# Last two weight pairs of a gated layer applied group by group, four weight conversions moved to earlier pairs

## The chip, the cores and the metric

The kernel runs on one core of one Trainium2 chip. The metric is the device time of one execution in microseconds (us). The kernel before takes 609.58 us, the median of three runs (609.0 to 614.15).

The engines are called by what they do: TensorE (PE in the rows; PEld is its loading of weights) multiplies matrices, VectorE (DVE), ScalarE (ACT) and GpSimd (POOL) work on elements, and SyncE (SP) starts transfers.

## The reference

Attention, a layer of eight experts and a gated layer follow one another. The change is in the last:

```python
def _moe2_ref(x, w_a, w_b, w_out) -> np.ndarray:
    a = x @ w_a
    b = x @ w_b
    return (a * b @ w_out).astype(np.float32)
```

`x` has 1536 tokens of 512, `w_a` and `w_b` are 512 x 1536, `w_out` is 1536 x 512. The weights come as float64 numbers.

## The kernel before

The attention and the experts fill the first 275 us or so of the span, and the change does not touch them. What follows is the gated layer.

**Numbers in two parts.** Each operand of a product is held as a high and a low part (`abh` and `abl` for the weights of a pair, `gh` and `gl` for the gated values, the even and odd `yw` tiles for tokens and for the last matrix). A product takes three matmuls for one: high by high, high by low, low by high.

**Pairs.** The inner width of 1536 is cut into 12 pieces of 128, `fc` from 0 to 11. A pair is the piece of `w_a` and the piece of `w_b`. `product(fc, g)` applies a pair to a third of the tokens (group `g`, 512 tokens): 24 matmuls of 128 x 512, first the `w_a` half, then the `w_b` half. Its lines are L1116 and L1117 (both with `abh`) and L1118 (with `abl`). ScalarE copies the first half out (`asb`, L1121), VectorE multiplies the second half by it (`gt`, L1122).

**Conversions.** `load_w` turns 128 x 512 weights from float64 into the two parts. It is a generator that is advanced a step at a time by `some(steps, n)` or to its end by `run(steps)`. Its steps are: issue the next transfer on SP's queue (L1006); `c_rest` on ScalarE (L1016) and `c_top` on VectorE (L1018, L1020); `c_ex` and `c_top` on VectorE (L1024, L1026); the high part on ScalarE (L1029), `c_ex` on VectorE (L1030), `c_rest` times `c_ex` on POOL (L1031); a subtraction on VectorE (L1033) and the low part on POOL (L1034). The step that ends a conversion and the first of the next one are made in one advance, so a conversion in a chain takes four. Two conversions make a pair (`load_ab`, both side by side); twelve make the last matrix (`load_c`, three chunks of four).

**Places.** The chunks of the last matrix go to the `yw` tiles: chunk 0 to tiles 6 and 7, which are free, chunk 1 to tiles 0 and 1, chunk 2 to 2 and 3. Tiles 0 and 1 hold the tokens of group 0, tiles 2 and 3 those of group 1, until the last product of that group is done.

**Order.** Everything here stands under a manual schedule: each engine executes in the order of the code. The loop over `fc` from 1 to 11 (L1158) makes three products, and behind each advances four steps of what pair `fc + 1` needs; from `fc + 1 = 8` on a conversion of chunk 0 is chained behind these. In the loop of `fc = 11` the eight conversions of chunks 1 and 2 begin behind the product of group 1.

**Last product.** It has 36 positions (`order`): for each a group and an `fc`. `split_g` makes `gh` on ScalarE (L1155) and `gl` on VectorE (L1156), two positions ahead; there are three buffers of each. Behind the split two steps of the remaining conversions are advanced, and then twelve matmuls stand on TensorE: L1185 and L1186 with `gh`, L1187 with `gl`, four times. Positions 0 to 15 are the groups 0 and 1 with chunks 0 and 1 of the last matrix (position 8 is the first that reads chunk 1), positions 16 to 23 the same groups with chunk 2, the last twelve are group 2.

Of the kernel before, what the change touches and what calls it, by code (L numbers as in the profile page):

```python
# [23 lines left out]
P = 128  # L24
# [37 lines left out]
def _consts():  # L62
    """Shape-only constants, one [128, n] float32 array; name -> (offset, width)."""
    p = np.arange(P)
# [37 lines left out]
def fused_kernel(  # L102
# [64 lines left out]

    # ---------------------------------------------------------------- expert blocks
    slots = [(0, i, wa_p) for i in range(NSA)]
    tick = [0]  # L170

    def take(dt, prefer=None):
        """A tile in the place that has been free for longest, of the pool that is preferred if it has any."""
        slots.sort(key=lambda t: t[:2])
        n = next((n for n, t in enumerate(slots) if t[2] is prefer), 0)
        _, i, pool = slots.pop(n)
        return (i, pool), pool.tile([P, CH], dt, name=f"w{i}")
# [6 lines left out]
    def gather_chunk(wi, c, prefer=None):  # L184
        """A chunk of an expert's weights, as it is."""
        place, r = take(F32, prefer)
        nc.gpsimd.indirect_dma_start(
            out=r, out_offset=None, in_=wt, in_offset=bass.IndirectOffsetOnAxis(ap=wi(c), axis=0))
        return place, r

    def parts(chunk, held, prefer=None):
        """Tiles for the two parts of a chunk, and what makes a piece of them."""
        place, r = chunk
# [32 lines left out]
    def gather(wi, ti, n, prefer=(None, None)):  # L226
        """What a block of n times 128 tokens needs."""
        ws = [gather_chunk(wi, c, prefer[0]) for c in range(2)]
        xgs = gather_x(xs, ti, n)
        return ws + [gather_chunk(wi, c, prefer[1]) for c in range(2, NCH)], xgs  # L230
# [53 lines left out]
    def block(ws, xgs, dst, **where):  # L284
        """A block by itself."""
        x = split_x(xgs, **where)
# [9 lines left out]
    def block_then(ready, dst, after, beside, prefer, after_prefer):  # L296
        """A block whose tokens and first chunks are ready, with what makes those of the block after it ready."""
        ws, w, x, held = ready
# [27 lines left out]
    def half_block(ready):  # L326
        """128 tokens: the tokens are stationary in the first product, and its result is turned."""
        ws, w, (xh, xl), held = ready
# [21 lines left out]

    # ---------------------------------------------------------------- attention and routing
    def rpool(stack, name, bufs):
# [160 lines left out]
    def first_max(L, n, O, key):  # L513
        """One-hot over E of the first largest of L ([P, n, E]); key: 8 less its place."""
        mx = r_p.tile([P, n], F32, name=f"mx{n}")
# [16 lines left out]
    def turned(b, t2):  # L532
        """The tokens of two tiles to DRAM, and turned."""
        x = xt2[b, t2]
# [10 lines left out]
    def partial_logits(b, t2):  # L545
        """Each part of the sum in 32 rows of its own."""
        pa = ps_b.tile([P, KD, P], F32, name="pl4", tag="b").rearrange("p c i -> p (c i)")[:, :2 * P]
# [16 lines left out]
    def prefix(b):  # L564
        """How many tokens of each expert come before each token."""
        O = oh[:, b * RB:(b + 1) * RB, :]
# [7 lines left out]
    def places(b):  # L574
        """Each token's place among those of its expert: unit of 128, and a row of ohl; in steps."""
        t0 = b * RB
# [19 lines left out]
    def count(t):  # L596
        """How many of the first t tiles' tokens each expert has."""
        pn = bank(E)
# [10 lines left out]
    def rows_of(key, out):  # L609
        """Rows of the weights of expert 8 - key."""  # L610
        w0 = r_p.tile([P, 1], F32, name="w0")
# [3 lines left out]
    def of_expert(name, vec, t0, n):  # L615
        """The entry of vec ([P, E]) of each token's expert."""
        t3 = r1.tile([P, n, E], F32, name=name + "3")
# [5 lines left out]
    def rows_y(tf, n, a, b):  # L623
        """Rows of the tokens tf (from 1; 0 for none) in ya and yb; those not there have row p, kept for that."""
        d = r1.tile([P, n], F32, name=f"d{n}")
# [17 lines left out]
    def early_expert():  # L643
        """A block of tokens of the first TE tiles, of the expert that has most of them."""
        ce = ear["ce"] = counted(ear["pc"], "ce")
# [45 lines left out]
    def tables(pc, pn, other):  # L691
        """The experts of the blocks, and which unit of which block each token has; other runs between."""
        full = ear["full"]
# [162 lines left out]
    def step(n):  # L856
# [3 lines left out]
        def due(ahead):  # L860
            """The pair that begins in so many steps (the first one's turn comes a step late)."""
            m = n + ahead
            return begin.get(0 if m == 1 else m) if m else None
# [80 lines left out]

    # ---------------------------------------------------------------- the other blocks
    nrun = nc.values_load(nmax[0:1, 0:1], min_val=0, max_val=NJ,
# [16 lines left out]

    # ---------------------------------------------------------------- second layer
    NG = 3
# [18 lines left out]
    def turn_y(g, ys):  # L984
        yh, yl = yt[g] = yw_tile(2 * g, [P, KD, GT]), yw_tile(2 * g + 1, [P, KD, GT])
        for c in range(KD):
# [5 lines left out]
            nc.vector.tensor_tensor(out=yl[:, c, :], in0=px, in1=f(yh[:, c, :]), op=ALU.subtract)  # L992

    loads = []
    for fc in range(KF2):
        loads += [(wab, 2 * fc + ab) for ab in range(2)]
        if fc >= KF2 - CH // RW:
            loads.append((wc, fc - KF2 + CH // RW))
    loads += [(wc, n) for n in range(CH // RW, KF2 * DM // RW)]
# [9 lines left out]
    def load_w(src, n, hi, lo):  # L1009
        """RW float64 weights, as the bits they come in, to the two parts of their float32 values; in steps."""  # L1010
        fetch()
# [34 lines left out]
    def run(steps):  # L1046
        for _ in steps:
            pass
# [21 lines left out]
    with tc.manual_schedule():  # L1070
# [86 lines left out]

        for fc in range(1, KF2):  # L1158
            steps = iter(())
            if fc + 1 < KF2:  # L1160
                steps = load_ab(fc + 1)
                if fc + 1 >= KF2 - CH // RW:
                    steps = chain(steps, load_c(0, fc + 1 - KF2 + CH // RW))
            for g in range(NG):
                product(fc, g, acc)
                if fc == KF2 - 1 and g > 0:
                    split_g(g - 1)
                some(steps, 4 if fc + 1 < KF2 else 3)
                if fc == KF2 - 1 and g == 0:
                    steps = chain(*(load_c(1, n) for n in range(CH // RW)), *(load_c(2, n) for n in range(CH // RW)))  # L1170
            if fc + 1 < KF2:
                run(steps)

# [21 lines left out]
def layout(q, k, v, moe_w_gate, moe_w1, moe_w2, moe2_w_a, moe2_w_b, moe2_w_out):  # L1195
    """The inputs as the kernel reads them: reordered, repeated and padded, nothing else."""
    f = np.float32
# [42 lines left out]
```

## Time and profile before

| what | us |
|---|---|
| median of three runs (lowest, highest) | 609.58 (609.0, 614.15) |
| span of the profiled execution, first to last instruction | 592.6 |
| whole time of the profiled execution | not on the page |
| TensorE busy in the span | 564.9 (95%) |
| VectorE busy | 391.0 (66%) |
| ScalarE busy | 236.5 (40%) |
| POOL busy | 226.8 (38%) |
| share of TensorE in the chain that ended last | 60% |
| share of VectorE in that chain | 8% |

The span is what the trace covers; the rest of the time lies around it. The busy shares are means over stages with different limits. A row of a timeline gives the start, the duration, the engine, the line and operation, and in brackets how long the engine had been idle before it and what it had waited for. Matmuls are pipelined: each is shown with some 0.39 us, but the next one starts 0.23 us later, so starts are compared.

### The profile page before, as it was taken

The page shows a single profiled execution, that of the slowest core. Times are in us where ns is not written, and L with a number is a line of the kernel's source. Part 1 is how long each engine was busy: PE and PEld are TensorE (multiplying, and loading weights), DVE is VectorE, ACT ScalarE, POOL GpSimd, SP SyncE. Part 2 cuts the span into 40 slices and gives each one's busy share as a digit, 9 for nine tenths or more (in the row PEclk, how much of TensorE's full clock was granted, in tenths as well). Part 3 has the DMA queues.
Part 4 walks back from the last instruction along what each step waited for, and adds up shares of the span by engine and source line. Part 5 has one row for each costly group of instructions (what it writes and reads, how often), then busy time and mean ns, then how long its engine had stood idle before and what let it go on. Part 6 is the DMA issues. An engine that isn't in the chain of part 4 may idle for free.

```text
span 592.6 us, 8797 instructions
## 1 busy us (share of the span) xinstructions
PE 564.9 (95%) x3166; PEld 475.0 (80%) x3166; DVE 391.0 (66%) x924; ACT 236.5 (40%) x500; POOL 226.8 (38%) x196
## 2 busy tenths in 40 slices
PE   5999998879999999999999999999999998999997
PEld 4999897768998998987888888888888876668885
DVE  4655578785878869766555555567898578883321
ACT  3566654314755756563422122212233233332221
POOL 4332236734455756730013344444544533430000
PEclk9999999879999999999999999999999999999999
DMA  9997947124977858654311122222332212201101
GB/s 232 246 230 191 241 139 280 72 105 136 384 270 312 304 207 310 234 203 162 112 64 35 44 72 71 72 71 72 107 107 76 67 56 87 72 0 72 71 1 71
DMA packets 24414, 83.85 MB, mean 141 GB/s; under 512 B 2992, under 2 KB 5552, under 8 KB 20784
## 3 DMA queue, kind: packets, MB, share of 16 engines
q1 hardware_dynamic: 14112, 38.16, 22.8%
q0 software_dynamic: 6944, 38.80, 17.3%
q10 hardware_dynamic: 3312, 6.29, 3.1%
q8 instruction: 26, 0.43, 0.3%
q14 instruction: 20, 0.16, 0.1%
HBM read 69.72 MB, written 12.32 MB: 138 GB/s over the span
## 4 chain that ended last, share of the span: by engine, by line
PE 60%; DVE 8%; issue 4%; ACT 1%; DMA 1%; SPq 0%; ACTq 0%; DVEq 0%
PE pa L1118 11%; PE pa L1116 11%; PE pa L1117 11%; PE po L1187 3%; PE po L1186 3%; PE po L1185 3%; PE py L253 3%; PE py L254 3%; PE py L252 3%; PE ph L277 2%; PE ph L278 2%; PE ph L279 2%; DVE w L205 2%; DVE gl L1156 1%; DVE c_top L1026 1%
## 5 line engine op out<-in xcount | busy, mean ns | idle before, releaser
L1116 PE MATMUL pa<-yw,abh 128*128 128x512 f32 x288 | 113.7, 395 | 0.0
L1118 PE MATMUL pa<-yw,abl 128*128 128x512 f32 x288 | 112.8, 392 | 0.0
L1117 PE MATMUL pa<-yw,abh 128*128 128x512 f32 x288 | 112.1, 389 | 0.0
L1031 POOL TENSOR_TENSOR c_rest<-c_rest,c_ex 128x512 f32<-128x512 f32 x36 | 54.7, 1531 | 147.0 <-DVE c_ex L1030 146.9
L205 DVE TENSOR_TENSOR w<-w,w 128x512 fp32r<-128x512 f32 x96 | 68.1, 752 | 5.4 <-ACT w L204 4.5
L1122 DVE TENSOR_TENSOR gt<-pa,asb 128x512 f32<-128x512 f32 x36 | 24.8, 690 | 63.0 <-PE pa L1118 55.9
L1118 PEld LDWEIGHTS pa<-yw,abl 128*128 128x128 f32 x288 | 54.0, 188 | 13.0 <-POOL abl L1034 0.9
L457 PE MATMUL s<-kt,qd 128*128 128x120 f32 x192 | 57.0, 445 | 7.2 <-DMA qd<-in_q 7.2
L1117 PEld LDWEIGHTS pa<-yw,abh 128*128 128x128 f32 x288 | 54.1, 188 | 11.4
L1187 PE MATMUL po<-yw,gl 128*128 128x512 f32 x144 | 58.1, 404 | 4.8 <-DVE gl L1156 4.8
L1116 PEld LDWEIGHTS pa<-yw,abh 128*128 128x128 f32 x288 | 54.1, 188 | 10.8
L457 PEld LDWEIGHTS s<-kt,qd 128*128 128x128 f32 x192 | 53.2, 367 | 10.1 <-POOL kt L449 7.8
L204 ACT CAST w<-w 128x512 fp32r<-128x512 f32 x96 | 54.4, 616 | 5.9 <-DVE w L205 3.0
L1185 PE MATMUL po<-yw,gh 128*128 128x512 f32 x144 | 56.7, 394 | 0.0
L1186 PE MATMUL po<-yw,gh 128*128 128x512 f32 x144 | 56.6, 393 | 0.0
L277 PE MATMUL ph<-xh,w 128*128 128x256 f32 x192 | 55.8, 291 | 0.3 <-PEq L948 0.3
L278 PE MATMUL ph<-xl,w 128*128 128x256 f32 x192 | 55.2, 287 | 0.0
L279 PE MATMUL ph<-xh,w 128*128 128x256 f32 x192 | 54.9, 286 | 0.0
L1156 DVE TENSOR_TENSOR gl<-gt,gh 128x512 fp32r<-128x512 f32 x36 | 29.6, 826 | 36.2 <-ACT gh L1155 36.2
L1121 ACT COPY asb<-pa 128x512 f32<-128x512 f32 x36 | 21.0, 583 | 56.8 <-PE pa L1118 56.8
L252 PE MATMUL py<-w,hh 128*128 128x512 f32 x104 | 41.8, 402 | 0.0
L253 PE MATMUL py<-w,hh 128*128 128x512 f32 x104 | 41.2, 396 | 0.6 <-DVE w L205 0.6
(200 smaller groups left out, 1088.2 us busy)
## 6 DMA issues: line engine op xcount, KB each, us to landing
raw<-in_wab SPq DMA_DIRECT2D x22, 512.0 KB, 4.4
raw<-in_wc SPq DMA_DIRECT2D x12, 512.0 KB, 3.5
vt<-in_v SPq DMA_DIRECT2D x8, 585.0 KB, 7.2
kr<-in_k SPq DMA_DIRECT2D x8, 400.0 KB, 7.2
vbt<-in_vb SPq DMA_DIRECT2D x8, 390.0 KB, 5.9
qd<-in_q SPq DMA_DIRECT2D x16, 192.0 KB, 6.1
xs<-x ACTq DMA_DIRECT2D x12, 256.0 KB, 4.5
yg<-ya SPq DMA_DIRECT2D x8, 256.0 KB, 3.3
```

What stands on the lines that cost most here:

```text
L205: nc.vector.tensor_tensor(out=l[:, c], in0=r[:, c], in1=f(a[:, c]), op=ALU.subtract)
L252: nc.tensor.matmul(py, a, b_, start=(fc == 0), stop=False)
L277: nc.tensor.matmul(ph, a, xh[:, c, :], start=(c == 0), stop=False)
L278: nc.tensor.matmul(ph, a, xl[:, c, :], start=False, stop=False)
L279: nc.tensor.matmul(ph, l, xh[:, c, :], start=False, stop=(c == KD - 1))
L457: nc.tensor.matmul(s[:, w, :], qs[b, c][:, :, 4 * t2 + w], kts[i][:, w, :], start=True, stop=True)
L1116: nc.tensor.matmul(pa, a, yh[:, c, :], start=(c == 0), stop=False)
L1117: nc.tensor.matmul(pa, a, yl[:, c, :], start=False, stop=False)
L1118: nc.tensor.matmul(pa, l, yh[:, c, :], start=False, stop=(c == KD - 1))
L1185: nc.tensor.matmul(po[g][i], a, bh, start=(fc == 0), stop=False)
L1186: nc.tensor.matmul(po[g][i], a, bl, start=False, stop=False)
L1187: nc.tensor.matmul(po[g][i], l, bh, start=False, stop=(fc == KF2 - 1))
```

## The change

Lines of the new kernel are one higher than the old ones from L994 on to L1157, and ten higher behind the changed loop: the subtraction L1033 is L1034 there, POOL's addition L1034 is L1035, `gt` is L1123, `gl` L1157.

The loop over `fc` ends at 9. The last two pairs, `f0 = 10` and `f1 = 11`, are applied in the order (10,0), (10,1), (11,0), (11,1), (10,2), (11,2) instead of pair by pair. The weights of pair 11 are converted from ahead of (10,0) to behind (10,1). The conversions of chunks 1 and 2 begin behind (11,0). The four conversions of chunk 0 move from pairs 8 to 11 to pairs 3, 5, 7 and 9. The number of instructions on each engine stays the same in this layer.

```diff
+    early_c = list(range(3, KF2 - 2, 2))
     loads = []
     for fc in range(KF2):
         loads += [(wab, 2 * fc + ab) for ab in range(2)]
-        if fc >= KF2 - CH // RW:
-            loads.append((wc, fc - KF2 + CH // RW))
+        if fc in early_c:
+            loads.append((wc, early_c.index(fc)))
...
-        for fc in range(1, KF2):
-            steps = iter(())
-            if fc + 1 < KF2:
-                steps = load_ab(fc + 1)
-                if fc + 1 >= KF2 - CH // RW:
-                    steps = chain(steps, load_c(0, fc + 1 - KF2 + CH // RW))
+        f0, f1 = KF2 - 2, KF2 - 1
+        for fc in range(1, f0):
+            steps = load_ab(fc + 1)
+            if fc + 1 in early_c:
+                steps = chain(steps, load_c(0, early_c.index(fc + 1)))
             for g in range(NG):
                 product(fc, g, acc)
-                if fc == KF2 - 1 and g > 0:
-                    split_g(g - 1)
-                some(steps, 4 if fc + 1 < KF2 else 3)
-                if fc == KF2 - 1 and g == 0:
-                    steps = chain(*(load_c(1, n) for n in range(CH // RW)), *(load_c(2, n) for n in range(CH // RW)))
-            if fc + 1 < KF2:
-                run(steps)
+                some(steps, 4)
+            run(steps)
+        steps = load_ab(f1)
+        some(steps, 2)
+        for g in range(2):
+            product(f0, g, acc)
+            some(steps, 2)
+        run(steps)
+        product(f1, 0, acc)
+        steps = chain(*(load_c(c, n) for c in (1, 2) for n in range(CH // RW)))
+        some(steps, 2)
+        product(f1, 1, acc)
+        some(steps, 4)
+        for n, fc in enumerate((f0, f1)):
+            product(fc, 2, acc)
+            split_g(n)
+            some(steps, 5)
```

How this moves instructions is seen at three places.

TensorE, kernel before, where the second product of pair 10 ends and the third begins (`abh_4852` and `abl_4853` are the parts of pair 10; `yw2` to `yw5` are the tokens of groups 1 and 2):

```order
L1116 MATMUL pa_5027<-yw2_3683,abh_4852 128x512
L1117 MATMUL pa_5027<-yw3_3684,abh_4852 128x512
L1118 MATMUL pa_5027<-yw2_3683,abl_4853 128x512
L1116 MATMUL pa_5057<-yw4_3758,abh_4852 128x512
L1117 MATMUL pa_5057<-yw5_3759,abh_4852 128x512
L1118 MATMUL pa_5057<-yw4_3758,abl_4853 128x512
```

TensorE, changed kernel, behind the same second product (`abh_4882` and `abl_4883` are the parts of pair 10, `abh_4972` and `abl_4973` those of pair 11; `yw0` and `yw1` are the tokens of group 0):

```order
L1117 MATMUL pa_5042<-yw2_3683,abh_4882 128x512
L1118 MATMUL pa_5042<-yw3_3684,abh_4882 128x512
L1119 MATMUL pa_5042<-yw2_3683,abl_4883 128x512
L1117 MATMUL pa_5062<-yw0_3602,abh_4972 128x512
L1118 MATMUL pa_5062<-yw1_3603,abh_4972 128x512
L1119 MATMUL pa_5062<-yw0_3602,abl_4973 128x512
```

The product that follows (10,1) now reads pair 11, where it read pair 10.

VectorE, kernel before, from the middle of the conversions of pair 11 to the end of pair 10 (`gt_3671` is pair 10; the last conversion of chunk 0 stands behind the two subtractions):

```order
L1030 TENSOR_SCALAR c_ex<-c_top 128x512 x2
L1122 TENSOR_TENSOR gt_3671<-pa,asb 128x512
L1033 TENSOR_TENSOR c_top<-c_top,abh 128x512 x2
L1018 TENSOR_SCALAR c_top<-raw 128x512
L1020 SCALAR_TENSOR_TENSOR c_top<-raw,c_top 128x512
L1024 TENSOR_SCALAR c_ex<-raw 128x512
L1026 SCALAR_TENSOR_TENSOR c_top<-c_ex,c_top 128x512
L1122 TENSOR_TENSOR gt_3671<-pa,asb 128x512
```

VectorE, changed kernel, the same conversions (`gt_3671` is pair 10, groups 0 and 1; `gt_3672` is pair 11):

```order
L1123 TENSOR_TENSOR gt_3671<-pa,asb 128x512
L1025 TENSOR_SCALAR c_ex<-raw 128x512
L1027 SCALAR_TENSOR_TENSOR c_top<-c_ex,c_top 128x512
L1025 TENSOR_SCALAR c_ex<-raw 128x512
L1027 SCALAR_TENSOR_TENSOR c_top<-c_ex,c_top 128x512
L1031 TENSOR_SCALAR c_ex<-c_top 128x512 x2
L1123 TENSOR_TENSOR gt_3671<-pa,asb 128x512
L1034 TENSOR_TENSOR c_top<-c_top,abh 128x512 x2
L1123 TENSOR_TENSOR gt_3672<-pa,asb 128x512
L1019 TENSOR_SCALAR c_top<-raw 128x512
L1021 SCALAR_TENSOR_TENSOR c_top<-raw,c_top 128x512
```

In both the two subtractions stand behind the `gt` of a product of group 1. Before, the next `gt` is that of pair 10 and group 2; now it is that of pair 11 and group 0, which needs what the subtractions make.

VectorE, kernel before, where the last pair ends and the last product begins (`gt_3672` is (11,2); the `gl` are those of positions 1 and 2):

```order
L1026 SCALAR_TENSOR_TENSOR c_top<-c_ex,c_top 128x512
L1122 TENSOR_TENSOR gt_3672<-pa,asb 128x512
L1156 TENSOR_TENSOR gl<-gt_3662,gh 128x512
L1030 TENSOR_SCALAR c_ex<-c_top 128x512
L1033 TENSOR_TENSOR c_top<-c_top,yw_5153 128x512
L1018 TENSOR_SCALAR c_top<-raw 128x512
L1020 SCALAR_TENSOR_TENSOR c_top<-raw,c_top 128x512
L1156 TENSOR_TENSOR gl<-gt_3663,gh 128x512
```

VectorE, changed kernel, the same place (the same names):

```order
L1025 TENSOR_SCALAR c_ex<-raw 128x512
L1027 SCALAR_TENSOR_TENSOR c_top<-c_ex,c_top 128x512
L1123 TENSOR_TENSOR gt_3672<-pa,asb 128x512
L1157 TENSOR_TENSOR gl<-gt_3662,gh 128x512
L1031 TENSOR_SCALAR c_ex<-c_top 128x512
L1034 TENSOR_TENSOR c_top<-c_top,yw_5091 128x512
L1019 TENSOR_SCALAR c_top<-raw 128x512
L1021 SCALAR_TENSOR_TENSOR c_top<-raw,c_top 128x512
L1025 TENSOR_SCALAR c_ex<-raw 128x512
L1027 SCALAR_TENSOR_TENSOR c_top<-c_ex,c_top 128x512
L1031 TENSOR_SCALAR c_ex<-c_top 128x512
L1157 TENSOR_TENSOR gl<-gt_3663,gh 128x512
```

Between the `gl` of positions 1 and 2 there were four operations of conversions, and there are seven.

## Rows read from the trace of the kernel before

**Rows 1.** Busy time of each engine by stretch (x instructions), clock, DMA share, GB/s.
```profile
463.30:479.60 16.30, 16.30 (x71) 13.39 (x72) 8.84 (x14) 6.54 (x12) 4.26 (x3) 1.00 0.21 63
479.60:530.60 51.00, 46.17 (x185) 33.36 (x184) 44.90 (x61) 15.52 (x28) 20.28 (x16) 1.00 0.17 53
```
**Rows 2.** Waits of TensorE from 275 to 592: total, times, longest.
```profile
PE po L1187 <- DVE gl L1156: 4.8, 14, 0.5
```
**Rows 3.** Timeline of TensorE: start, duration, engine, line, operation.
```profile
462.61 0.40 PE L1116 MATMUL pa<-yw,abh 128*128 128x512 f32 x1
...
463.26 0.50 PE L1118 MATMUL pa<-yw,abl 128*128 128x512 f32 x1
...
468.42 0.39 PE L1116 MATMUL pa<-yw,abh 128*128 128x512 f32 x1
...
479.37 0.39 PE L1185 MATMUL po<-yw,gh 128*128 128x512 f32 x1
...
485.86 0.50 PE L1187 MATMUL po<-yw,gl 128*128 128x512 f32 x1 [0.41 <-DVE gl L1156]
...
529.90 0.50 PE L1187 MATMUL po<-yw,gl 128*128 128x512 f32 x1 [0.46 <-DVE gl L1156]
```
**Rows 4.** The chain that ended last, in order of time: last product.
```profile
587.99 0.25 PE po L1187
```
**Rows 5.** Timeline of all engines: the end of a pair's conversion, and later `gt`.
```profile
442.34 0.69 DVE L1122 TENSOR_TENSOR gt<-pa,asb 128x512 f32<-128x512 f32 x1 [0.50 <-ACT asb L1121]
442.95 2.39 DVE L1033 TENSOR_TENSOR c_top<-c_top,abh 128x512 f32<-128x512 f32 x2
...
444.76 2.99 POOL L1034 TENSOR_TENSOR abl<-c_top,c_rest 128x512 fp32r<-128x512 f32 x2
...
446.55 0.50 PE L1118 MATMUL pa<-yw,abl 128*128 128x512 f32 x1
...
468.69 0.69 DVE L1122 TENSOR_TENSOR gt<-pa,asb 128x512 f32<-128x512 f32 x1 [0.42 <-PE pa L1118]
...
479.64 0.69 DVE L1122 TENSOR_TENSOR gt<-pa,asb 128x512 f32<-128x512 f32 x1 [2.10 <-ACT gh L1155]
```
**Rows 6.** Timeline of VectorE and POOL in the last product.
```profile
475.33 0.42 DVE L1018 TENSOR_SCALAR c_top<-raw 128x512 int32<-128x512 int32 x1
...
485.12 0.68 DVE L1156 TENSOR_TENSOR gl<-gt,gh 128x512 fp32r<-128x512 f32 x1
485.72 0.41 DVE L1024 TENSOR_SCALAR c_ex<-raw 128x512 int32<-128x512 int32 x1
...
489.24 0.68 DVE L1033 TENSOR_TENSOR c_top<-c_top,yw 128x512 f32<-128x512 f32 x1
...
490.06 1.35 POOL L1034 TENSOR_TENSOR yw<-c_top,c_rest 128x512 fp32r<-128x512 f32 x1 [1.29 <-DVE c_top L1033]
...
490.29 1.67 DVE L1020 SCALAR_TENSOR_TENSOR c_top<-raw,c_top 128x512 int32<-128x512 int32 x1
...
495.99 0.68 DVE L1033 TENSOR_TENSOR c_top<-c_top,yw 128x512 f32<-128x512 f32 x1
...
530.37 2.38 DVE L1156 TENSOR_TENSOR gl<-gt,gh 128x512 fp32r<-128x512 f32 x2
```
**Rows 7.** By stretch, as rows 1; the third figure from the end is the clock.
```profile
104.50:105.00 0.50, 0.32 (x2) 0.32 (x3) 0.00 (x0) 0.50 (x2) 0.20 (x1) 0.61 1.00 381
...
108.00:108.50 0.50, 0.50 (x9) 0.10 (x1) 0.50 (x2) 0.00 (x0) 0.09 (x1) 0.97 0.00 0
...
121.00:122.00 1.00, 0.00 (x0) 0.00 (x0) 0.93 (x3) 0.00 (x0) 1.00 (x2) 0.84 0.00 0
...
128.00:129.00 1.00, 1.00 (x9) 1.00 (x8) 0.09 (x1) 0.38 (x1) 0.69 (x2) 0.75 0.50 82
```
**Rows 8.** Timeline of TensorE: the first products after two waits.
```profile
104.68 1.97 PE L237 MATMUL px<-cs,xg 128*128 128x128 f32 x8 [0.76 <-ACT xt L543]
...
122.64 0.20 PE L569 MATMUL prb<-oh,tri 128*128 128x48 bf16 x1 [5.69 <-DVE oh L521]
```

## The prediction

> **What bounds the kernel now.** I first read the busy time by stretch. From 463.30 to 479.60 (the last weight pair) TensorE is busy 16.30 of 16.30 us, VectorE only 8.84; from 479.60 to 530.60 (the first part of the last matrix product) TensorE is busy 46.17 of 51.00 and VectorE 44.90 [rows 1]. So the products of the weight pairs are TensorE's, with room on VectorE, and the stretch after them is VectorE's. The list of waits names the place: L1187, a product with the low half `gl`, waits for VectorE's L1156 14 times [rows 2]. TensorE's timeline gives the size. The last product phase begins at 479.37, the 183rd matmul of it, the one of position 15 that needs its `gl`, starts at 529.90, and the last one (the 432nd) at 587.99 [rows 3, 4]. After 529.90 nothing waits: 58.09 us for 249 matmuls is 0.233 each and 2.80 for a position of twelve. At that pace the first 182 would take 42.5 us; they take 50.53. So 8.0 us are lost in 14 waits, 0.57 each, and nothing else in this part is to be won.
>
> VectorE is late there because between two `gl` stands half a conversion of the last matrix (eight conversions are left at 475.33, the last ends at 530.37). A period of one conversion and two `gl` runs from 489.24 to 495.99, 6.75 us, against 5.60 for two positions [rows 6].
>
> I write (fc,g) for the product of pair fc and token group g, S, Q and Z for TensorE's starts of (11,0), of (10,2) and of position 0, all in the changed order.
>
> **Part one: the weights of pair 11 lose their cover.** Before, three products of pair 10 stand ahead of the first product of pair 11; the last part of a conversion (VectorE L1033, then POOL L1034, which writes `abl`) follows the second product's `gt` on VectorE, and the third product hides it. In the change (11,0) follows (10,1) directly, and the subtraction still stands behind `gt` of (10,1), which waits for that very product's last matmul. So TensorE must wait, by this chain from S. `gt` starts 0.27 after the next product's start (468.69 against 468.42); the subtraction starts 0.61 later (442.95 against 442.34) [rows 3, 5]; POOL's addition starts 0.82 after that (490.06 against 489.24) and takes 1.35 [rows 6]; the matmul starts 0.29 after its end (half of 2.99 after 444.76 is 446.26, the matmul comes at 446.55) [rows 5]. That is S + 3.34. Without a wait it is the third matmul, at S + 0.46. With 0.10 for the slower matmul after a wait (0.50 us against 0.40) the loss is 2.98. Before, the same place loses 463.26 - 462.61 - 0.46 + 0.10 = 0.29 [rows 3]. POOL has finished both earlier products by then, since `c_ex` is now made right behind `gt` of (10,0). **Term one: +2.7**; from +2.5 (no slower matmul, subtraction at once) to +3.3 (POOL still holds VectorE up, as the pair of subtractions at 442.95 that takes 2.39 instead of 1.36 [rows 5]).
>
> **Part two: four conversions go to pairs 3, 5, 7 and 9.** They lay in the products of pairs 7 to 10, three conversions to 16.4 us, and lie there again, with lighter loops between. TensorE covers them; without that cover each would cost what it costs at the end. Zero, to +0.5 if the waits of 0.29 come at more loop starts than now. Their DMAs and those of the last eight conversions stay in one order on SP's queue, each a conversion ahead, as before; nothing new waits behind them.
>
> **Part three: the last eight conversions start earlier.** Each has four steps. Before, six of their 33 are issued ahead of position 0, now sixteen, so 17 remain for positions 0 to 8, and `gl`(10) is the last with conversion work ahead of it instead of `gl`(15). What one costs: from 475.33 to 530.37 there are 55.04 us, less a wait of 2.10 for a product, with eight conversions, fifteen `gl` at 0.60 (485.12 to 485.72) and one `gt` at 0.61; that leaves 5.42 for a conversion [rows 5, 6]. In the change VectorE is free to run on only from `gt` of (11,1), at Q + 0.27, because until then it waits for TensorE's `gt` twice. From there to `gl`(10) it has three `gt` (1.8), eleven `gl` (6.6), and eight conversions less the two operations done before and the subtraction left over (43.4 - 1.7 = 41.7): 50.1 in all. `gl`(10) then ends at Q + 50.4. Two products are 10.95 (479.37 - 468.42) [rows 3], so this is Z + 39.5. Going step by step instead, between Q and Z stand nine steps (two conversions and a quarter, 12.2), two `gt` and `gl`(0), 14.0 in 10.95, so `gt` of (11,2) comes at Z + 3.3, `gl`(1) is ready at Z + 4.5, and behind five more steps `gl`(2) at about Z + 11.6. Eight positions at 3.375 (half of 6.75) add 27.0: Z + 38.6. I take the mean, Z + 39.0. From position 10 to 15 TensorE needs 5 x 2.80 = 14.0, and stands at Z + 53.0 where the old kernel stood at 50.5. **Term two: +2.5.** The five waits fewer (2.9 us) are more than paid back by one of about 4 us at position 2 and one of about 1 us at position 1, where VectorE comes with a backlog.
>
> The bounds of it. Above: `gt` and `gl` in full and the first wait longer, +4. Below: in the loops of three conversions and three `gt` each takes at most (16.4 - 1.8) / 3 = 4.87, so eight could be 4.4 us cheaper: -2. I keep near 5.42, since in the bursts, too, VectorE and POOL alternate: L1020 at 490.29 takes 1.67 and ends 0.55 after POOL's L1034 (490.06 + 1.35) [rows 6].
>
> The Trainium skill, "SBUF — State Buffer", section "SBUF: two separate sides", states that VectorE operations with two SBUF inputs and GpSimd operations lock one shared pair of ports and that the loser blocks for the whole instruction. By that rule, a conversion cannot shrink where VectorE has nothing else to do, and term two is +2.5 rather than -2; the row at 490.29 agrees with it, and it speaks against packing conversions together.
>
> **Part four: the clock.** A wait of about 3 us is new to this stretch. Earlier in this execution the granted clock fell to 0.5 (1.2 GHz) near 104.7, after a thin stretch that ends with a gap of 0.76, and was back at 108.0; and again at 121.8, in a gap of 5.69, and was back near 128.5 [rows 7, 8]. No row shows what one gap of 3 us does. Bounds: nothing, or 6.7 us at half pace, 3.3. The first fall is the nearer row: 3.4 us at half pace would lose 1.7, less what falls inside the gap itself. **Term three: +1.3**, in (11,0). A second fall near position 2 would be hidden: there TensorE waits 0.57 at each of the eight positions that follow.
>
> **Sum.** 2.7 + 2.5 + 1.3 = 6.5 on a span of 592.6. The page gives no whole time of the profiled execution; the median of the runs, 609.58, lies 17.0 above the span, and I leave these 17.0 as they are: 616.1.
>
> **The rivals.** (a) The clock does not fall: 609.6 + 2.7 + 2.5 = 614.8. For it: a single gap; against it: the fall near 104.7. (b) Conversions cost 4.87 in the bursts: 609.6 + 2.7 - 2.0 + 1.3 = 611.6. For it: the loops; against it: 490.29. (c) The change does what its order suggests: VectorE reaches position 0 without a backlog and keeps up after it. It decides if a conversion and two `gl` take at most 5.60, two positions. Then all 8.0 are won, and with term one 604.3 remains, faster than before. Against it stands the period of 6.75, and the 14.0 us that VectorE has to do in the 10.95 from Q to Z. (d) The clock stays low through two products, or term two is at its upper bound: 609.6 + 2.7 + 4 + 3.3 = 619.6.
>
> **How the numbers follow.** The forecast has 0.50, (a) 0.20, (b) 0.12, (c) 0.06, (d) 0.12. The range from 611.5 to 619.5 leaves out (c) and the ends. About 1% (6.1 us) is what a measurement of this kernel can tell from no change: slower by more means over 615.7, which the forecast just does in some two thirds of its cases, and (d): 0.47. Within 1%: the rest of the forecast, (a), (b) and most of (c): 0.50. Faster by over 1%: 0.03.
>
> **What would show it.** Step one: L1119 of (11,0) waits about 2.9 us for POOL's `abl`; if it waits under 1 us, the chain is wrong. Step three: a wait of 3 to 5 us at position 2, then waits of some 0.57 that end at position 10, near Z + 39.0; if TensorE stands at position 10 by Z + 34, term two has the wrong sign. Step four: a granted clock below 1.00 within a few us of (11,0). The loops of pairs 2 to 9 should show TensorE busy throughout. If the waits of `gl` vanish altogether, (c) holds and the prediction is wrong.

## The result, and the profile after

The changed kernel takes 617.31 us (median of four executions, 614.12 to 618.61), the kernel before beside it 610.12 (609.0 to 614.15): a ratio of 1.0102, with a 95% interval from 1.0053 to 1.0151. It is slower, by 6.2 us by that ratio and by 7.2 between the medians; the interval reaches from 3.2 to 9.2 us. The forecast was 616.1, 6.5 slower.

The profiled execution took 617.39 us, 1.8 more than its span of 615.6. The span is 23.0 longer than that of before, and most of the 23.0 has nothing to do with the change: the first product of a weight pair starts at 293.19 in the trace after and at 277.82 in the trace before. So I compare the gated layer alone, from the start of that first matmul to the start of the last one of the last matrix. TensorE's timeline, before:

```profile
277.82 0.48 PE L1116 MATMUL pa<-yw,abh 128*128 128x512 f32 x1
...
587.83 0.40 PE L1187 MATMUL po<-yw,gl 128*128 128x512 f32 x1
```

After:

```profile
293.19 0.48 PE L1117 MATMUL pa<-yw,abh 128*128 128x512 f32 x1
...
499.59 0.39 PE L1195 MATMUL po<-yw,gh 128*128 128x512 f32 x1
...
610.84 0.40 PE L1197 MATMUL po<-yw,gl 128*128 128x512 f32 x1
```

(The 587.99 of [rows 4] is a row of the chain; in the timeline the same matmul starts at 587.83.) Before the layer takes 310.01 us: 201.55 up to Z, the start of position 0, and 108.46 from Z on. After it takes 317.65: 206.40 up to Z, which is at 499.59, and 111.25 from Z on. Of the 4.85 more ahead of Z, 0.9 lie at its start, where TensorE waits for the tokens; this wait varies from execution to execution (0.9, 0.3 and 0.7 us in the three traces that have it). So 3.95 come ahead of Z and 2.79 behind it, 6.7 in all.

The page after, its parts 1 and 4 (busy time with its share of the span, and the chain that ended last):

```profile
PE 570.9 (93%) x3166; PEld 480.6 (78%) x3166; DVE 390.9 (63%) x924; ACT 236.8 (38%) x500; POOL 223.9 (36%) x196
...
PE 61%; DVE 6%; issue 4%; DMA 2%; ACT 2%; another core or an unknown queue 0%; SPq 0%; POOL 0%; ACTq 0%; DVEq 0%; POOLq 0%
```

VectorE does the same work in the same number of instructions; nothing in these sums shows where the time went. The list of TensorE's waits from 275 on (total, times, longest), which answers to [rows 2]:

```profile
PE po L1195 <- ACT gh L1156: 3.9, 1, 3.9
PE po L1197 <- DVE gl L1157: 3.6, 7, 1.2
PE pa L1119 <- POOL abl L1035: 2.7, 1, 2.7
```

The 14 waits for `gl` (4.8 us) have become seven (3.6), but two single waits of 3.9 and 2.7 are new. (The lines have moved by one in the converter, L1034 to L1035, and by ten in the last product, L1187 to L1197.) The new wait ahead of Z, in the timeline of all engines (start, duration, engine, line, operation, the idle time before it and what ended it):

```profile
473.06 0.39 PE L1117 MATMUL pa<-yw,abh 128*128 128x512 f32 x1
...
473.33 0.69 DVE L1123 TENSOR_TENSOR gt<-pa,asb 128x512 f32<-128x512 f32 x1 [1.95 <-PE pa L1119]
473.94 1.28 DVE L1034 TENSOR_TENSOR c_top<-c_top,abh 128x512 f32<-128x512 f32 x2
474.79 2.80 POOL L1035 TENSOR_TENSOR abl<-c_top,c_rest 128x512 fp32r<-128x512 f32 x2 [1.01 <-DVE c_top L1034]
...
476.40 0.50 PE L1119 MATMUL pa<-yw,abl 128*128 128x512 f32 x1 [2.72 <-POOL abl L1035]
```

S is 473.06. `gt` of (10,1), the subtraction, POOL's addition and the matmul follow at S + 0.27, + 0.88, + 1.73 and + 3.34. Then the clock (windows: length, busy time of PE, PEld, DVE, ACT, POOL with the number of instructions, the granted clock, the DMAs' share, GB/s):

```profile
478.00:481.00 3.00, 3.00 (x9) 2.33 (x8) 0.00 (x0) 1.16 (x2) 0.00 (x0) 0.50 0.00 0
...
484.00:499.40 15.40, 15.40 (x69) 12.63 (x69) 11.05 (x16) 4.77 (x9) 3.92 (x3) 1.00 0.20 56
499.59:550.59 51.00, 43.53 (x173) 32.64 (x172) 40.05 (x54) 14.73 (x26) 17.87 (x13) 0.97 0.14 44
```

From 478 to 481 TensorE is busy all the time and runs nine matmuls where thirteen go at full speed: the granted clock is 0.50 (1.2 GHz). By 484 it is back. The last window has the length of the second one of [rows 1], counted from Z: 43.53 us of matmuls instead of 46.17. The waits there, in TensorE's timeline:

```profile
504.18 0.50 PE L1197 MATMUL po<-yw,gl 128*128 128x512 f32 x1 [1.24 <-DVE gl L1157]
...
510.65 0.50 PE L1195 MATMUL po<-yw,gh 128*128 128x512 f32 x1 [3.88 <-ACT gh L1156]
...
511.91 0.70 PE L1197 MATMUL po<-yw,gl 128*128 128x512 f32 x1 [0.53 <-DVE gl L1157]
...
525.41 0.50 PE L1197 MATMUL po<-yw,gl 128*128 128x512 f32 x1 [0.49 <-DVE gl L1157]
...
538.91 0.50 PE L1197 MATMUL po<-yw,gl 128*128 128x512 f32 x1 [0.46 <-DVE gl L1157]
```

They lie at position 1 (504.18), position 2 (510.65, 511.91) and then at positions 6 to 10, the last at Z + 39.3. What is late is seen in the timelines of VectorE, ScalarE and POOL:

```profile
484.47 0.69 DVE L1021 SCALAR_TENSOR_TENSOR c_top<-raw,c_top 128x512 int32<-128x512 int32 x1
488.85 0.69 DVE L1123 TENSOR_TENSOR gt<-pa,asb 128x512 f32<-128x512 f32 x1 [3.69 <-PE pa L1119]
...
502.84 0.68 DVE L1123 TENSOR_TENSOR gt<-pa,asb 128x512 f32<-128x512 f32 x1
...
506.48 1.33 POOL L1035 TENSOR_TENSOR yw<-c_top,c_rest 128x512 fp32r<-128x512 f32 x1
...
506.72 1.64 DVE L1021 SCALAR_TENSOR_TENSOR c_top<-raw,c_top 128x512 int32<-128x512 int32 x1
...
509.45 0.62 ACT L1030 CAST yw<-c_top 128x512 fp32r<-128x512 f32 x1 [5.31 <-DVE c_top L1027]
509.98 0.61 ACT L1156 CAST gh<-gt 128x512 fp32r<-128x512 f32 x1
...
510.62 1.23 DVE L1157 TENSOR_TENSOR gl<-gt,gh 128x512 fp32r<-128x512 f32 x1 [0.74 <-ACT gh L1156]
...
539.38 2.37 DVE L1157 TENSOR_TENSOR gl<-gt,gh 128x512 fp32r<-128x512 f32 x2
```

VectorE waits from 485.16 to 488.85, 3.69 us, for the product whose `gt` comes next in its order; then it reaches `gt` of (11,2) only at Z + 3.25. At position 2 even the high half `gh` is late, although ScalarE only copies it: ahead of it on ScalarE stands L1030 of a conversion, which waited 5.31 us for VectorE. So VectorE's backlog reaches TensorE through two engines. The same operation L1021 takes 0.69 at 484.47, and 1.64 at 506.72, where POOL's addition (1.33 us from 506.48) runs beside it. The last row is `gl`(11), the first behind all conversion work.

### The profile page after: what moved, and what is told of

Its sections match the earlier page's. It is cut to its first block, busy times and chain, and to the rows that moved or that the text cites. A ratio compares the mean times of both kernels' runs of the same rounds, so it can differ in the third digit from the quotient of the medians.

```text
span 615.6 us, 8799 instructions
## 1 busy us (share of the span) xinstructions
PE 570.9 (93%) x3166; PEld 480.6 (78%) x3166; DVE 390.9 (63%) x924; ACT 236.8 (38%) x500; POOL 223.9 (36%) x196
## 4 chain that ended last, share of the span: by engine, by line
PE 61%; DVE 6%; issue 4%; DMA 2%; ACT 2%; another core or an unknown queue 0%; SPq 0%; POOL 0%; ACTq 0%; DVEq 0%; POOLq 0%
PE pa L1119 10%; PE pa L1117 10%; PE pa L1118 10%; PE po L1197 4%; PE po L1196 4%; PE po L1195 4%; PE ph L279 3%; PE ph L277 3%; PE py L253 3%; PE ph L278 3%; PE py L252 3%; PE py L254 3%; DMA yg<-ya 1%; DVE gl L1157 1%; DVE c_top L1019 1%
## 5 line engine op out<-in xcount | busy, mean ns | idle before, releaser
L205 DVE TENSOR_TENSOR w<-w,w 128x512 fp32r<-128x512 f32 x96 | 65.9, 732 | 4.4 <-ACT w L204 2.9
L1123 DVE TENSOR_TENSOR gt<-pa,asb 128x512 f32<-128x512 f32 x36 | 24.8, 690 | 59.4 <-PE pa L1119 54.9
L1197 PE MATMUL po<-yw,gl 128*128 128x512 f32 x144 | 58.2, 404 | 3.6 <-DVE gl L1157 3.6
L1195 PE MATMUL po<-yw,gh 128*128 128x512 f32 x144 | 57.5, 399 | 3.9 <-ACT gh L1156 3.9
L1157 DVE TENSOR_TENSOR gl<-gt,gh 128x512 fp32r<-128x512 f32 x36 | 28.6, 796 | 45.3 <-ACT gh L1156 45.3
L1196 PE MATMUL po<-yw,gh 128*128 128x512 f32 x144 | 57.2, 397 | 0.0
L277 PEld LDWEIGHTS ph<-xh,w 128*128 128x128 f32 x192 | 37.6, 196 | 13.6 <-DVE hl L281 8.3
L252 PE MATMUL py<-w,hh 128*128 128x512 f32 x104 | 42.3, 407 | 0.0
L281 DVE SCALAR_TENSOR_TENSOR hl<-ph,hh 128x256 fp32r<-128x256 f32 x48 | 20.0, 419 | 34.1 <-ACT hh L280 23.4
```

The source lines that it names most:

```text
L205: nc.vector.tensor_tensor(out=l[:, c], in0=r[:, c], in1=f(a[:, c]), op=ALU.subtract)
L252: nc.tensor.matmul(py, a, b_, start=(fc == 0), stop=False)
L277: nc.tensor.matmul(ph, a, xh[:, c, :], start=(c == 0), stop=False)
L1195: nc.tensor.matmul(po[g][i], a, bh, start=(fc == 0), stop=False)
L1196: nc.tensor.matmul(po[g][i], a, bl, start=False, stop=False)
L1197: nc.tensor.matmul(po[g][i], l, bh, start=False, stop=(fc == KF2 - 1))
```

## The experiments

The times of one kernel spread over up to 11 us, and the traces differ most ahead of the layer. So beside the times I give the length of the layer in each trace, measured as above, with its parts ahead of Z and behind it. The kernel before was timed again beside the experiments: 615.18 us (25 executions) beside e1_cover, e2_pace and e3_split, 615.13 (11 executions) beside e4_all, a2_after, e5_early and e6_late, where it took 610.12 beside the first timing of the change. So times are compared with those, as a ratio with its 95% interval in brackets.

| kernel | layer | ahead of Z | from Z on |
|---|---|---|---|
| before | 310.01 | 201.55 | 108.46 |
| c_before | 311.25 | 202.81 | 108.44 |
| after | 317.65 | 206.40 | 111.25 |
| a2_after | 317.14 | 205.90 | 111.24 |
| e1_cover | 312.16 | 200.95 | 111.21 |
| e2_pace | 312.81 | 205.58 | 107.23 |
| e3_split | 315.25 | 204.02 | 111.23 |
| e4_all | 301.30 | 201.66 | 99.64 |
| e5_early | 309.51 | 201.05 | 108.46 |
| e6_late | 322.35 | 211.10 | 111.25 |

Two theories of the 2.8 us behind Z are set against each other. A: what counts is the sum of VectorE's work up to the last `gl` that has conversion work ahead of it. B: what counts is the burst around Z, that is, the backlog with which VectorE comes to positions 1 and 2.

**c_before: the kernel before, unchanged.**

> The kernel before, unchanged, looked at again. The profile of before had a span of 592.6 us, while its runs took 609.0 to 614.15; in the changed kernel the whole time is only 1.8 us longer than the span. If the first profile simply shows a faster execution of the part ahead of the gated layer, this one has a span near 608, with the difference ahead of the first product of a pair, and the gated layer (first matmul of a pair to last matmul of the kernel) again takes about 310.0 us. If instead the gated layer itself is slower in the timed runs, it takes some 325 us here.

It took 617.69 us with a span of 615.9 (expected near 608), so a whole time lies 1.8 above its span, and not 17.0. The execution profiled before was simply a fast one ahead of the layer, which starts there at 277.82 and here at 299.88. The mean granted clock of the span is 0.99 there and 0.97 here, so some of this goes with the clock; how much is not shown. One of the waits that are new ahead of the layer (the list of TensorE's waits of c_before):

```profile
PE ph L277 <- DVE hl L281: 8.0, 5, 2.7
```

The layer itself is the same from Z on (108.44 against 108.46). Ahead of Z it has 1.3 us more, with a stretch of low clock that began before the layer's first product (3.4 us from 299.2 on). So the layer can be compared from trace to trace to a few tenths behind Z, and ahead of Z where no such stretch lies.

**e1_cover: one product put back between the conversion and its user.**

```diff
         steps = load_ab(f1)
-        some(steps, 2)
-        for g in range(2):
-            product(f0, g, acc)
-            some(steps, 2)
+        some(steps, 4)
+        product(f0, 0, acc)
         run(steps)
+        product(f0, 1, acc)
         product(f1, 0, acc)
```

The conversion of pair 11 is now issued to its end behind (10,0), and (10,1) covers it.

> The changed kernel, with the conversions of pair 11 two steps further ahead: their subtractions and POOL additions now stand behind the gt of (10,0) and not behind that of (10,1). My theory (term one and the clock): the wait of 2.9 us in (11,0) goes, and with it the clock's fall there, so the time falls from 617.3 to about 613.0, the waits at positions 1 and 2 stay. Rival: POOL or VectorE is what is late, and the wait moves to the second half of (11,0) or to (11,1); then the time stays within 1 us of 617.3.

Measured: 617.96 us (614.83 to 621.6), 1.0049 [1.0016, 1.0082] of before. The 613.0 were missed as a time, since before, too, took 5 us longer beside it; against before it is 3.0 us by the ratio, and 613.0 against 610.1 is 2.9. TensorE's timeline has no wait in (11,0) any more; those at positions 1 and 2 are as after, and a window over the end of the pairs is full at clock 1.00:

```profile
465.00:495.00 30.00, 30.00 (x134) 24.76 (x132) 19.20 (x30) 7.28 (x14) 9.49 (x7) 1.00 0.16 53
```
```profile
501.64 0.50 PE L1196 MATMUL po<-yw,gl 128*128 128x512 f32 x1 [1.23 <-DVE gl L1157]
...
508.11 0.79 PE L1194 MATMUL po<-yw,gh 128*128 128x512 f32 x1 [3.88 <-ACT gh L1156]
```

A second window, over position 2 and what follows it, has a low clock, about 6.8 us at 0.50 (10 x 0.34 / 0.50):

```profile
506.00:516.00 10.00, 7.85 (x23) 5.82 (x24) 8.34 (x13) 4.45 (x8) 3.92 (x3) 0.66 0.33 106
```

Ahead of Z the layer takes 200.95, 5.45 less than after (4.6 without the 0.9 at its start), and from Z on it is the same to 0.04 us. So the missing cover makes the wait in (11,0), and without the wait no fall of the clock is seen there in this trace; the time behind Z is another matter.

**e2_pace: one step of a conversion per position instead of two.**

```diff
             split_g(n + 2)
-            some(steps, 2)
+            some(steps, 1)
```

> The changed kernel, with one step of the remaining conversions per position of the last product and not two (17 steps remain, so they end at position 16 instead of 8). My theory (conversion work ahead of a gl is what TensorE waits for): the waits of positions 3 to 10 go, those at positions 1 and 2 stay, as the backlog is made before position 0; position 10 is reached about Z + 35 to 36 instead of Z + 39.3, and the time falls to 613 to 614. Rival: the last matrix's later chunks come too late at this pace, and TensorE waits at positions 16 to 19 for yw tiles; then the time is 617 or more.

Measured: 617.57 us (612.28 to 623.56), 1.0047 [1.0003, 1.009]. The 613 to 614 were missed as a time; against before it is 2.9 us by the ratio, for an expected 3 to 4. The rival's time came, but not its waits at positions 16 to 19. From Z on the layer takes 107.23, 4.0 less than after and 1.2 less than before. TensorE's timeline has two waits left there; two windows show the clock around the second and the stretch behind it, which is full:

```profile
506.45 0.50 PE L1197 MATMUL po<-yw,gl 128*128 128x512 f32 x1 [1.24 <-DVE gl L1157]
...
512.92 0.76 PE L1195 MATMUL po<-yw,gh 128*128 128x512 f32 x1 [3.90 <-ACT gh L1156]
```
```profile
510.00:520.00 10.00, 7.00 (x23) 5.20 (x24) 9.12 (x14) 4.00 (x7) 2.95 (x3) 0.83 0.23 63
...
515.00:560.00 45.00, 45.00 (x193) 36.36 (x193) 25.01 (x42) 13.84 (x23) 11.78 (x9) 0.98 0.08 24
```

The waits at positions 1 and 2 are what they were after, to 0.02 us, and yet 4.0 us are gone: the work that VectorE no longer has to do ahead of `gl`(10). The product with that `gl` starts at Z + 35.4 and not at Z + 39.3. That speaks for A.

**e3_split: the splits of positions 0 to 2 together behind (10,2).**

```diff
             product(fc, 2, acc)
-            split_g(n)
+            if n == 0:
+                for m in range(3):
+                    split_g(m)
             some(steps, 5)
 ...
-            split_g(n + 2)
+            if n:
+                split_g(n + 2)
```

The `gl` of positions 0, 1 and 2 are made ahead of the ten conversion steps that stand behind (10,2) and (11,2); the sum of the work is the same.

> The changed kernel, with the splits of positions 0, 1 and 2 all made behind (10,2), ahead of the ten steps that stand there, so that no gl is late at positions 1 and 2; two steps per position as before. Theory A (VectorE's sum of work up to the last gl with conversions ahead of it decides): the waits move to positions 3 to 5, position 10 is reached at Z + 39 to 40 all the same, and the time stays within 1 us of 617.3. Theory B (the burst ahead of positions 1 and 2 is itself the loss, about 5 us): position 10 is reached at about Z + 34, and the time falls to about 612.

Measured: 622.24 us (616.35 to 626.25), 1.0095 [1.0052, 1.0139]. As a time that is 5 us over what was expected under A; against before it is 5.8 us by the ratio, and the change was 6.2. TensorE's timeline:

```profile
484.68 0.50 PE L1119 MATMUL pa<-yw,abl 128*128 128x512 f32 x1 [2.72 <-POOL abl L1035]
...
518.51 0.79 PE L1198 MATMUL po<-yw,gh 128*128 128x512 f32 x1 [3.89 <-ACT gh L1156]
...
521.83 0.79 PE L1200 MATMUL po<-yw,gl 128*128 128x512 f32 x1 [2.09 <-DVE gl L1157]
...
545.59 0.50 PE L1200 MATMUL po<-yw,gl 128*128 128x512 f32 x1 [0.46 <-DVE gl L1157]
```

The waits at positions 1 and 2 are gone, and larger ones stand at position 3; position 10 still waits for its `gl`, at Z + 39.3 (545.59, Z is 506.29). From Z on the layer takes 111.23, after 111.25. B falls: the burst only chooses the position at which the time is lost. This trace has a second use. The same gap is in (11,0) (484.68), but the clock did not fall behind it; it fell behind the waits of position 3:

```profile
486.00:490.00 4.00, 4.00 (x19) 3.31 (x18) 0.00 (x0) 1.15 (x2) 0.00 (x0) 1.00 0.00 0
...
516.00:530.00 14.00, 9.39 (x26) 6.99 (x27) 12.76 (x18) 4.32 (x8) 5.17 (x4) 0.63 0.27 79
```

So term one alone is 204.02 - 200.95 (e1_cover) = 3.07, and the fall of the clock alone is 205.58 (e2_pace, which has it) - 204.02 = 1.56.

**e4_all: the cover, the early splits, and a pace that TensorE can hide.** The edits of e1_cover and e3_split, and:

```diff
-            some(steps, 5)
+            some(steps, 1 if n else 3)
 ...
-            some(steps, 2)
+            some(steps, 1 if n % 4 else 2)
```

> The changed kernel with three things at once: pair 11 converted two steps earlier (as in the run that covers its last step), the splits of positions 0 to 2 made behind (10,2), and the conversions spread: three steps and one step behind (10,2) and (11,2), then five steps for four positions. Theory (conversion work ahead of a gl, and nothing else, is what TensorE waits for): per four positions VectorE has 1.25 conversions of 5.42 and four gl of 0.60, 9.2 us, against 11.2 on TensorE, so no wait is left; the pair products take about 201.0 from their first matmul, the last product 432 x 0.233 = 100.5 and not 111.2, the layer 301.5 against 310.0 to 311.3 of before and 317.65 of the change; the time is 8 to 9 us below that of before on the same chip. Rival: the eight conversions do not fit at all, the last chunk is late and TensorE waits at positions 16 to 19 for yw; then the layer takes 306 or more.

Measured: 603.93 us (600.93 to 608.82), 0.9844 [0.9794, 0.9893] of before; it is faster than both kernels. By the ratio it is 9.6 us below before (11.2 between the medians), for an expected 8 to 9. Ahead of Z the layer takes 201.66, 0.7 of it the wait for the tokens; from Z on it takes 99.64, 8.8 less than before. The list of TensorE's waits is empty from 440 on, and the windows over the last pairs and the last product are full:

```profile
450.00:475.00 25.00, 25.00 (x111) 20.54 (x110) 20.56 (x32) 7.63 (x13) 13.39 (x9) 1.00 0.23 71
475.00:500.00 25.00, 25.00 (x112) 20.62 (x111) 14.36 (x21) 6.82 (x13) 8.69 (x6) 1.00 0.17 61
500.00:540.00 40.00, 40.00 (x176) 32.67 (x175) 32.68 (x48) 14.86 (x25) 14.11 (x10) 1.00 0.22 66
```

So the new order can run the last product at TensorE's pace. What VectorE has to do is spread over the positions up to 17 (the last conversion's addition on POOL starts 49.7 us after Z) instead of lying ahead of position 10. The three edits stand together here: behind Z the cover alone gave nothing (e1_cover), the early splits alone nothing (e3_split), a slower pace alone 4.0 us (e2_pace).

Whether the earlier places are needed for this gain is not shown: no run spreads the conversions in the kernel before. An estimate from its rows leaves room for it. There 27 steps remain from position 0 on, and the last piece of the last matrix is read at position 19. One and a half steps per position would be 1.5 x 5.42 / 4 + 0.60 = 2.6 us on VectorE, against 2.80 on TensorE.

**a2_after: the changed kernel again, beside e4_all.**

> The changed kernel again, unchanged, beside before on the same chip, since the time ahead of the gated layer differs from run to run by some us. The three terms: the pair products take 204.0 without and 205.6 with a fall of the clock in (11,0), the last product 111.2 against 108.4; so the layer is 5.2 to 7.0 us longer than before (310.0 to 311.3), and the time is above that of before by the same.

Measured: 620.96 us (617.31 to 622.39), 1.0105 [1.0064, 1.0145]; the layer takes 317.14, with the same gap in (11,0), 3.10 from one matmul's start to the next, and the same fall of the clock. The result stands, and so does the place.

**e5_early: in the kernel before, only the four conversions moved.**

```diff
+    early_c = list(range(3, KF2 - 2, 2))
 ...
-        if fc >= KF2 - CH // RW:
-            loads.append((wc, fc - KF2 + CH // RW))
+        if fc in early_c:
+            loads.append((wc, early_c.index(fc)))
 ...
-                if fc + 1 >= KF2 - CH // RW:
-                    steps = chain(steps, load_c(0, fc + 1 - KF2 + CH // RW))
+                if fc + 1 in early_c:
+                    steps = chain(steps, load_c(0, early_c.index(fc + 1)))
```

> The kernel before with only the four conversions of chunk 0 moved to pairs 3, 5, 7 and 9; order of the products, places and the last phase as before. My step (covered by TensorE, price zero, between -0.6 and +0.5): the layer takes 309.5 to 311.5 us, as before; the last product 108.4. Rival: the earlier conversions take VectorE or POOL time that the pairs 2 to 9 need, and TensorE waits there; then the pair products take over 202.5.

Measured: 613.34 us (one execution); the layer takes 309.51, with 108.46 from Z on as before and 201.05 ahead of it, 0.5 less than before. By itself the move costs nothing, and it takes away the small waits that pairs 10 and 11 had. The waits behind Z are those of [rows 2]:

```profile
PE po L1188 <- DVE gl L1157: 4.8, 14, 0.5
```

**e6_late: in the changed kernel, the four conversions put back to four pairs in a row.**

```diff
-    early_c = list(range(3, KF2 - 2, 2))
+    early_c = list(range(7, KF2 - 1))
```

They are one pair earlier than in the kernel before, because the last loop over all groups ends one pair earlier.

> The changed kernel with the four conversions of chunk 0 put back late, with pairs 7 to 10 (as close to the old places as the new loop allows). If the early places matter to the result, the layer changes by more than 1.5 us; by my step it does not: pair products 204 to 206 (by the clock), the last product 111.2, the layer 315.2 to 317.6, with the 2.9 us wait in (11,0).

Measured: 623.53 us (one execution); the layer takes 322.35, 4.7 more than after, or 5.6 more without the wait for the tokens that after has. This expectation was missed. All of it lies ahead of Z (TensorE's timeline, and a window):

```profile
447.38 0.50 PE L1119 MATMUL pa<-yw,abl 128*128 128x512 f32 x1 [0.43 <-POOL abl L1035]
...
475.70 0.50 PE L1117 MATMUL pa<-yw,abh 128*128 128x512 f32 x1 [0.86 <-ACT abh L1030]
...
481.34 0.80 PE L1119 MATMUL pa<-yw,abl 128*128 128x512 f32 x1 [4.91 <-POOL abl L1035]
```
```profile
480.00:490.00 10.00, 8.66 (x26) 6.91 (x27) 0.63 (x2) 1.17 (x2) 2.51 (x2) 0.66 0.00 0
```

The wait in (11,0) grows from 2.72 to 4.91 us, two more stand ahead of it, and the clock stays low for longer, some 6.8 us (10 x 0.34 / 0.50). VectorE's timeline shows what is late:

```profile
473.19 0.68 DVE L1123 TENSOR_TENSOR gt<-pa,asb 128x512 f32<-128x512 f32 x1
...
477.17 0.69 DVE L1123 TENSOR_TENSOR gt<-pa,asb 128x512 f32<-128x512 f32 x1 [0.50 <-ACT asb L1122]
477.78 2.38 DVE L1034 TENSOR_TENSOR c_top<-c_top,abh 128x512 f32<-128x512 f32 x2
```

These are `gt` of (10,0), `gt` of (10,1) and the subtractions of pair 11. After, both `gt` waited for TensorE, that of (10,1) for 1.95 us; here the first waits for nothing, since VectorE itself is late. With three conversions in the loop of pair 9 it comes late to pair 10, and the conversion of pair 11, which has only two products of pair 10 to lie in, is late with it: `gt` of (10,1) comes at S + 1.47 (S is 475.70) instead of S + 0.27, and the subtractions behind it take 2.38 instead of 1.28. Part of the time is the clock's; the trace does not part it cleanly from the waits.

## Why the prediction was right, and where it was not

**Bound of the kernel before.** Right: the last product's first part is VectorE's, and with the steps spread out it becomes TensorE's (e4_all). The 8.0 us that I saw to win there were 8.8 in e4_all. (I took the last matmul's start as 587.99; with 587.83 the same working gives 8.2.)

**Part one** came out to the hundredth, `abl` at S + 3.34, and the mechanism is the one foretold, but the hundredth is luck: POOL starts 0.85 behind the subtraction for 0.82 and takes 1.40 for 1.35, and the matmul follows 0.21 later for 0.29. Term one is 3.07 for 2.98. What I set against it, the 0.29 that before loses at the same place, was too small: before also loses some 0.25 in (10,0), so that 0.6 go (201.55 - 200.95). By e5_early, where both are gone as well, some 0.5 of this comes from the moved conversions and not from the order of the products.

**Part two** had the right price, zero or a little less (e5_early, -0.5), and half of a reason. I wrote that TensorE covers the conversions, as if it did so wherever they lie. In the new order it does so in the early pairs; next to the last pairs they cost some 5 us (e6_late, one execution). The move is not an addition beside the reordering, it is what makes room for it.

**Part three** is the main point, and it held. Position 10 is the last that waits, at Z + 39.3 for Z + 39.0; `gt` of (11,2) comes at Z + 3.25 for Z + 3.3. Term two is 2.8 for 2.5. The price of 5.42 us for a conversion holds in the bursts too: from `gt` of (11,1) at 488.85 to 539.38 are 50.53 us; less three `gt` (1.8) and eleven `gl` (6.6), and with the two operations done before (1.1) added, 43.2 are left for eight conversions, 5.40 each. Rival (b), which had 4.87, falls. The reason given for it is seen again: L1021 takes 0.69 alone and 1.64 beside POOL's addition, and ends at 508.36, 0.55 after it (506.48 + 1.33). By the Trainium skill, "SBUF — State Buffer", section "SBUF: two separate sides", the loser of the shared ports blocks for the whole instruction. Here, too, the trace agrees. Three details were off. I expected the wait of 4 us at position 2 on `gl`; it came on `gh`, through ScalarE's queue. I had a wait at each of the positions 3 to 10; in the trace none stands at 3 to 5. And the cause of the loss is broader than the burst at Q that I described: e3_split shows that the sum up to `gl`(10) sets it, as my first way of working it out (Q + 50.4) had it.

**Part four.** The clock fell in (11,0), which costs 1.56 us (e2_pace against e3_split), predicted 1.3. Rival (a), that it would not, is what e3_split did, with the same gap: it is open from one execution to the next, and that it fell in the profiled execution of the change was not certain beforehand. A second fall, near position 2, is hidden, as said: from Z on, e1_cover and e3_split, each with a longer one, take what after takes, to 0.04 us.

**Sum.** 3.07 + 1.56 - 0.6 + 2.8 = 6.8, against 6.7 in the trace and 6.5 foretold. That the times differ by 6.2 is no finer a confirmation than their interval, 3.2 to 9.2, allows. **The step that failed** is the last one: "the median of the runs, 609.58, lies 17.0 above the span, and I leave these 17.0 as they are". Around a span lie 1.8 us (c_before, and every other profiled execution); by that the profiled execution of before would have taken 594.4, below every timed one, and the other 15.2 were a fast execution ahead of the layer. It did no harm, because only the difference was carried over to the median, but had the change touched the part ahead of the layer, I would have costed it in an execution that was not typical.

**Rival (c)**, VectorE keeps up, asked for a conversion and two `gl` in 5.60 us. They still took 6.75 after the change (two such periods from 525.41 to 538.91). e4_all reaches what (c) hoped for by another way: less conversion work per position, not cheaper work.

## What to carry to other kernels

Making places free sooner did not help here until what fills them was also spread over more of the time that the bound engine offers. Add up the slower engine's work ahead of the last operand that it delivers late, because here that sum set the end, and the order within it only chose where the wait was seen. A product that is moved from between a conversion and its user was the cover of that conversion: follow the chain from the instruction that the converter queues behind, here one matrix product and 2.9 us. And if a profiled execution's span is far from the median, find out where before using it as a base; a stretch measured from one event to another agreed to 0.02 us in two traces of the kernel before (108.46 and 108.44) whose spans differ by 23.

## What the runs showed of the hardware

A gap of 3.11 us from one matmul's start to the next, otherwise at full pace, was followed by a granted clock of 0.5 in three traces (after, a2_after, e2_pace) and by none in a fourth (e3_split). The fall cost 1.56 us (e2_pace against e3_split). What decides between the two is not shown.

In the last product, where TensorE waits for VectorE again behind it, a longer fall of the clock cost nothing more: after has one of about 3.1 us there (51 x 0.03 / 0.50), and about 6.8 us at 0.50 in e1_cover and 10.4 in e3_split (14 x 0.37 / 0.50) left the length from Z on what it was after, to 0.04 us. In e2_pace, where no such wait follows, the fall seems to have cost its full price. From Z on it takes 7.59 us more than e4_all; its two long gaps (1.63 and 4.29 from one matmul's start to the next, against 0.23) make 5.46 of it, and the 2.1 that are left go with 3.4 us at 0.50 (10 x 0.17 / 0.50), which alone would cost 1.7.

The part ahead of the layer took from 277.8 (before) to 302.3 us (e3_split) in these traces, in kernels whose code is the same there. The profiled execution of before was at the fast end by 15 us or more.
